# A written-out order of some 4,400 steps: the centroids' normalisation split into its single instructions, and the first 700 entries put in another order

## The chip, the cores and the metric

The kernel runs on one core of one Trainium2 chip, as one program and one launch. The metric is the time of one execution on the device, in microseconds (us), as the median of several runs.

The engines are called as in the profile: PE is TensorE, DVE is VectorE, ACT is ScalarE, POOL is GpSimd, and SP is SyncE, which here issues every transfer between memory and the chip.

## The reference

What is computed is an attention whose queries see only keys of the same cluster, and behind it a layer with a rational function between two matrix products. Cut to what matters:

```python
q_n, k_n, c_n = (each row divided by its norm + 1e-6)            # centroids: 8 heads x 16 clusters x 64
q_assign = argmax(q_n @ c_n.T);  k_assign = argmax(k_n @ c_n.T)  # per head
scores = q @ k.T / 8, -1e9 where q_assign != k_assign            # 4 batches, 8 heads, 768 x 768
x = softmax(scores) @ v                                          # heads side by side: 3072 x 512
h = x @ w_in                                                     # 512 -> 2048
g = (a0 + a1 h + a2 h^2 + a3 h^3) / (1 + |b0||h| + |b1|h^2 + 1e-6)
out = g @ w_out                                                  # 2048 -> 512
```

## The kernel before

Heads are worked in pairs: 4 batches of 4 pairs. For a pair, `prep` loads q and k, scales them by powers of two, splits them into a high and a low half of 16 bits (tiles `tk1`, `tq1`), turns them (`sk1`, `sq1`), multiplies them with the centroids (`ptl`), and finds each row's cluster as a one-hot row (`mx`, `df`, `mxi`, `oh`). The one-hot rows go into second tiles (`tk2`, `tq2`), which are turned too (`sk2`, `sq2`); a score is one product of the first tiles plus one of the second. For the pair 0 of batch 0 PE does the turning; for the others a transfer does.

Batch 0 works in `attend_keys`: a first pass of scores (`s`) gives each row's maximum (`top`, one DVE reduction over 768 values for each of 12 score tiles of a pair), a second pass (`z`) gives the scores with keys in rows, exponentials go to `at`, and `px` is the product with the values (tile `rv`). During batch 0 the two weight matrices are also loaded in 32 pieces (`rwi`, `rwo`), decoded on ACT (`mwi`, `gwi`, ...) and DVE (`wwi`, `wwo`), given their sign on POOL, scaled and split (`win`, `wout`). Behind that come the matrix products of the layer (`ph`, `po`) of one batch beside the attention of the next.

The centroids come once, ahead of all: one load (`craw`), squares and their sum (`csq`, `css`), a logarithm and an exponential on ACT, two steps of a root iteration and a division on DVE (`cn`, `cr`, `cnrm`), a turn on PE (`ctp`), and three instructions that write the parts of 16 bits (`cen`) that `ptl` reads.

Nothing is scheduled at run time. Each step calls `op(...)`, which only adds its function to a list; the table `ORDER` (line 63) names the places of that list, and `emit` calls them in that order. So each engine gets its instructions, and SP its transfers, in the order of the table. A step with several instructions, as the normalisation's, can't be parted by the table. The number that stands beside each engine's name in `op` is not used by it.

Each engine works off its own row and waits where a tile is not ready. Raw weights, and the values for their largest entry (`rvm`), share two buffers; `rk` and `rq` have one each, so that a pair's keys are loaded when the pair before has read its own.

"Warm" groups (`warm`, 16 of 8 products of 128x128 on a constant tile) have no result that is used; they are entries of the table like others.

Of the kernel before, what the change touches and what calls it, by code (L numbers as in the profile page):

```python
# [19 lines left out]
P = 128  # L20
# [42 lines left out]
72 73 4424 4421 4423 74 75 4435 4427 76 40 41 42 43 44 45 4429 4425 4422 371 370 373 4436 4428 375 376 4430  # L63
369 368 374 3 4 5 377 382 383 384 389 378 379 6 4434 380 381 385 386 387 388 390 397 12 13 392 393 400 77 34
35 36 38 37 39 7 8 9 4432 4426 399 398 394 396 402 391 395 10 11 28 29 30 31 401 403 404 32 33 519 518 521 523
524 405 46 50 47 48 525 530 406 531 407 532 408 516 517 522 526 527 528 4431 49 51 537 538 529 372 66 70 67
410 533 534 535 536 540 411 413 412 409 414 416 78 79 415 539 68 69 71 541 52 53 80 81 542 82 83 419 420 417
418 421 422 643 644 545 646 431 648 84 85 86 546 649 54 423 55 87 544 88 89 14 15 642 641 647 16 17 424 427
428 547 548 650 655 441 656 549 442 657 662 429 430 443 90 550 551 444 432 445 91 552 553 543 554 433 437 438
434 651 446 447 425 426 652 448 18 520 1 19 20 92 93 56 57 462 463 466 467 468 469 449 450 663 451 21 22 464  # L70
653 654 452 658 110 111 112 659 465 113 114 115 439 440 435 436 660 453 454 455 661 456 60 62 63 457 458 104
105 106 459 108 107 109 665 666 470 471 472 460 461 556 555 557 558 473 667 474 122 123 124 480 482 481 483
569 570 125 126 127 484 485 23 24 561 562 575 576 0 670 116 25 117 118 119 664 120 121 565 566 498 499 500 501
671 672 673 674 669 26 2342 2343 94 573 574 486 487 58 27 675 676 128 129 668 677 678 679 571 572 475 567 568
# [12 lines left out]
264 265 244 807 245 246 214 247 815 816 808 266 267 268 212 269 270 1358 1356 216 217 252 272 250 720 721 722
248 271 273 604 809 810 1357 734 735 723 724 829 830 1359 831 1360 274 275 276 832 770 833 1361 834 1362 835
175 277 1363 736 737 2 278 279 210 1366 1367 750 294 298 295 1364 296 297 299 725 748 749 751 726 727 738 739
740 741 1365 742 251 752 753 1368 754 755 280 281 836 843 743 306 310 1369 61 179 282 283 728 729 744 284 285  # L90
332 254 213 333 334 135 307 308 309 837 841 842 844 211 745 215 1497 335 336 337 338 339 340 341 342 312 313
314 315 316 290 317 756 757 758 855 856 838 1370 1371 1372 1373 1374 759 343 286 344 760 1375 345 1376 1377
839 840 857 858 859 761 762 763 1495 300 301 304 1496 1501 1498 1500 302 303 1296 1297 845 846 860 847 1379
1378 1382 1380 1502 861 862 346 1503 1505 347 1504 1506 1507 1508 1509 253 848 873 311 305 318 319 849 348 877
292 293 1513 1514 1510 287 1511 1512 320 321 874 288 289 875 876 322 323 1515 291 349 350 351 352 353 354 1516
355 356 324 1298 1299 863 864 878 325 357 358 850 851 852 359 360 361 879 880 1383 1381 1387 1388 1395 1396
865 866 328 1389 326 249 1390 327 1391 867 329 1397 1392 1393 764 765 1398 1399 881 882 883 884 885 868 869
870 1403 1404 362 363 364 853 854 1400 1401 1300 1301 1518 1517 1519 1520 365 366 367 1521 1522 1405 1302 1303
1304 886 887 1411 1412 1305 1306 1645 1644 1647 1649 1406 1407 888 1650 871 1523 1524 1413 1307 1308 1414 1415
255 1309 1310 1408 1409 1394 1351 1402 1416 1417 1410 1643 1418 1642 1384 891 892 893 894 330 1651 1653 1431  # L100
1432 1311 1433 897 898 899 1423 1424 895 896 1312 1313 1314 1434 900 901 902 1435 903 904 1315 1316 1526 1317
1385 1386 907 908 910 909 911 1654 912 1436 1437 331 1655 1425 923 924 925 746 1426 1427 926 927 928 929 913
914 1428 1429 940 941 943 942 1648 915 1430 1499 1447 1448 1449 905 933 747 872 930 1318 1525 944 945 1439
1440 916 946 947 1319 1652 917 1419 1420 1421 1422 1450 1451 1656 1657 1441 1442 1443 918 2346 1452 1527 2344
1453 1454 889 1444 973 974 976 956 948 1660 931 975 919 920 1445 1529 1459 1460 1461 1658 932 1661 977 978
1462 1463 957 959 1467 1468 960 1464 1465 921 906 979 980 934 935 936 1469 949 950 1470 1471 958 989 990 992
991 622 937 1472 962 963 961 995 996 1475 1476 1477 1659 1662 1473 1478 964 922 993 994 951 1479 1480 1005
1006 1007 1483 1484 1485 1663 1481 952 953 1008 1009 1486 1487 1010 1446 2345 1438 1455 1456 1457 1458 938 939
1488 1489 981 965 966 967 982 1011 1530 1466 1528 1534 1535 1536 954 1542 1543 1544 1664 968 969 970 890 983
1537 1538 2347 1665 1666 1667 1668 1669 1320 2348 1482 1545 1546 984 1539 1540 1547 1548 1026 1027 1028 1029  # L110
1030 1031 997 1032 1042 1043 1045 998 1044 1550 1551 1552 1558 1559 1560 1046 999 1000 1553 1554 1012 1670
1033 1531 985 986 1561 1532 1533 1555 1556 1059 1060 1062 1063 1562 1047 971 1048 1049 1490 955 972 1791 1789
1793 1549 1792 1794 1563 1013 1034 1061 1015 1065 1671 1673 1570 1571 1572 1035 1564 1064 1001 1573 1574 1474
1491 1492 1493 1586 1587 1014 1494 1036 1575 1576 1588 1108 1109 1796 1797 988 1111 1112 1050 1589 1590 1798
1800 1801 1790 1795 1037 1578 1579 1591 1592 1799 1113 1066 1067 1052 1541 1565 1672 1321 1322 1593 1676 1674
1677 1557 1577 1646 1580 1323 1581 1002 1124 1051 1125 1127 1582 1583 1802 1324 1016 1017 1018 1019 1110 1053
1606 1607 1608 1068 987 1003 1584 1128 1038 1039 1609 1610 1594 1595 1126 1803 1611 1612 1129 2349 1596 1075
1076 1078 1077 1069 1325 1070 1597 1598 1130 1131 1054 1055 1056 1599 1807 1614 1615 1616 1804 1081 1082 1617
1004 1091 1092 1094 1079 1805 1600 1080 1618 1619 1020 1022 1093 1326 1327 1114 1328 1329 1330 1808 1622 1623
1624 1097 1098 1115 1625 1566 1567 1620 1806 1809 1095 1096 1626 1627 1021 1675 1681 1682 1683 2350 1024 1684  # L120
1099 1601 1585 1628 1613 1629 1071 1072 1101 1685 1810 1141 1142 1630 1631 1041 1040 1686 1687 1083 1568 1569
1084 1085 1116 1143 1147 1689 1690 1331 1144 1145 1146 1086 1100 1102 2394 1812 1811 1691 1692 1693 1103 1632
# [1742 lines left out]
```

## Time and profile before

| | |
|---|---|
| median of 3 runs | 882.0 us (881.77 to 883.29) |
| the profiled execution | 883.15 us, of which 881.4 us are its span from the first to the last instruction |
| PE busy | 856.7 us (97% of the span) |
| DVE busy | 814.1 us (92%) |
| ACT busy | 783.9 us (89%) |
| POOL busy | 516.9 us (59%) |

The shares are averages over stages with different limits. The change lies in the first 131 us of the span, so what counts is which engine sets the pace there; a busy PE is not PE at its peak, since ends of matmuls are modelled.

### The profile page before, as it was taken

How to read it: one execution, taken by the hardware profiler on the slowest of the kernel's cores; microseconds unless marked ns; L12 is line 12 of the kernel's file. 1: busy time of each engine (PE TensorE's matmuls, PEld its weight loads, DVE VectorE, ACT ScalarE, POOL GpSimd, SP SyncE). 2: the span in 40 equal slices, each digit the busy share in tenths (PEclk: the TensorE clock that was granted, in tenths of full speed). 3: DMA queues.
4: the chain of work that ended last, by engine and by line, in shares of the span. 5: the costliest groups of instructions: out<-in, count | busy, mean ns of one | idle time of the engine just before them, and what ended most of it. 6: DMA issues, size and time to landing. Idle time of an engine off the chain costs nothing.

```text
span 881.4 us, 20941 instructions
## 1 busy us (share of the span) xinstructions
PE 856.7 (97%) x7893; PEld 595.3 (68%) x7893; DVE 814.1 (92%) x1627; ACT 783.9 (89%) x1482; POOL 516.9 (59%) x515
## 2 busy tenths in 40 slices
PE   7799999989999999999999999999999999999997
PEld 6577777757666676676766666676766666766654
DVE  6999998999999999999999999999999997879784
ACT  7698899999999999999999999999998988875752
POOL 3433445447687666667667566657674755345563
PEclk8899999999999999999999999999999999999999
DMA  7898757849989999889799999988987984330000
GB/s 230 238 244 196 188 178 198 177 94 204 174 155 180 197 164 186 172 141 228 162 182 202 172 179 183 157 177 155 167 152 142 146 154 78 76 59 1 25 25 25
DMA packets 353014, 135.77 MB, mean 154 GB/s; under 512 B 327824, under 2 KB 344208, under 8 KB 352912
## 3 DMA queue, kind: packets, MB, share of 16 engines
q1 hardware_dynamic: 352912, 134.42, 75.3%
q8 instruction: 62, 1.02, 0.5%
q14 instruction: 40, 0.33, 0.1%
HBM read 41.98 MB, written 6.29 MB: 55 GB/s over the span
## 4 chain that ended last, share of the span: by engine, by line
PE 52%; DVE 20%; ACT 17%; issue 6%; POOL 4%; DMA 0%; SPq 0%; ACTq 0%; DVEq 0%; POOLq 0%
PE po L1772 18%; PE ph L1623 18%; PE s L1254 6%; PE px L1334 5%; ACT s L420 4%; DVE s L1283 3%; DVE ah L1314 3%; ACT u L420 3%; ACT ah L420 3%; DVE top L1407 2%; ACT at L420 1%; DVE s L1742 1%; ACT t L420 1%; DVE t L1641 1%; PE ptl L1149 1%
## 5 line engine op out<-in xcount | busy, mean ns | idle before, releaser
L1623 PE MATMUL ph<-x,win 128*128 128x256 f16 x2304 | 267.5, 274 | 2.4 <-DVE t L1648 2.4
L1772 PE MATMUL po<-wout,g 128*128 128x512 f16 x1152 | 265.6, 379 | 0.0
L1623 PEld LDWEIGHTS <-win 128*128 128x128 f16 x2304 | 224.7, 98 | 43.2 <-DVE t L1648 4.2
L1772 PEld LDWEIGHTS <-g 128*128 128x128 f16 x1152 | 111.5, 98 | 120.8 <-issue 2.4
L1761 POOL TENSOR_TENSOR g<-t,u 128x512 f16<-128x512 f32 x84 | 113.1, 1348 | 82.8 <-DVE t L1754 52.0
L1314 DVE SCALAR_TENSOR_TENSOR ah<-s,su,ah 128x768 f16<-128x768 f32 x144 | 143.6, 1012 | 6.9 <-ACT ah L420 6.0
L1283 DVE TENSOR_SCALAR_CACHE_REDUCE s<-s,cc 128x768 f32<-128x768 f32 x144 | 144.5, 1018 | 5.0 <-PE s L1254 4.4
L420 ACT ACTIVATE ah<-s,su 128x768 f16<-128x768 f32 x144 | 126.4, 896 | 11.1 <-DVE su L1302 10.2
L420 ACT ACTIVATE s<-s,nm 128x768 f32<-128x768 f32 x144 | 125.9, 874 | 9.9 <-DVE s L1283 8.6
L1254 PE MATMUL s<-sk,sq 128*128 128x384 f16 x576 | 113.7, 326 | 2.3 <-DVE ah L1314 1.7
L1688 POOL TENSOR_TENSOR s<-s,u 128x512 f32<-128x512 f32 x69 | 91.6, 1332 | 31.9 <-ACT s L420 28.2
L1254 PEld LDWEIGHTS <-sq 128*128 128x128 f16 x576 | 53.0, 99 | 45.1 <-DVE ah L1314 12.8
L1334 PE MATMUL px<-at,vhi 128*64 128x256 f16 x864 | 73.7, 275 | 0.1
L1641 DVE SCALAR_TENSOR_TENSOR t<-ph,gk,t 128x512 f32<-128x512 f32 x84 | 62.3, 742 | 5.4 <-ACT t L420 5.2
L420 ACT ACTIVATE t<-ph,gk 128x512 f32<-128x512 f32 x84 | 65.1, 776 | 2.3 <-PE ph L1623 2.3
L1648 DVE SCALAR_TENSOR_TENSOR t<-t,gk,ph 128x512 f32<-128x512 f32 x84 | 62.2, 742 | 2.0 <-ACT u L420 0.8
L1742 DVE SCALAR_TENSOR_TENSOR s<-s,g 128x512 f32<-128x512 f32 x84 | 61.1, 727 | 1.1 <-POOL g L1717 0.5
L420 ACT ACTIVATE u<-ph,gk 128x512 f32<-128x512 f32 x84 | 57.5, 686 | 4.6 <-PE ph L1623 1.9
L420 ACT ACTIVATE u<-s,cq 128x512 f32<-128x512 f32 x84 | 60.1, 721 | 0.0
L1334 PE MATMUL px<-at,vlo 128*64 128x256 f16 x432 | 59.8, 273 | 0.0
L1748 POOL TENSOR_TENSOR t<-t,s 128x512 f32<-128x512 f32 x28 | 37.7, 1345 | 34.4 <-DVE s L1742 26.8
L1334 PEld LDWEIGHTS <-vhi 128*64 128x64 f16 x864 | 45.4, 110 | 12.3 <-issue 7.3
(237 smaller groups left out, 1572.8 us busy)
## 6 DMA issues: line engine op xcount, KB each, us to landing
rwo<-in_moe_w_out_dram SPq DMA_DIRECT2D x16, 512.0 KB, 4.0
rwi<-in_moe_w_in_dram SPq DMA_DIRECT2D x16, 512.0 KB, 4.1
rk<-in_k_dram SPq DMA_DIRECT2D x32, 192.0 KB, 3.8
rq<-in_q_dram SPq DMA_DIRECT2D x32, 192.0 KB, 3.8
rvm<-in_v_dram SPq DMA_DIRECT2D x16, 384.0 KB, 4.0
rv<-in_v_dram SPq DMA_DIRECT2D x16, 384.0 KB, 4.4
out_dram<-ob SPq DMA_DIRECT2D x24, 256.0 KB, 2.9
sq<-sq SPq DMA_DIRECT2D x12, 192.0 KB, 3.5
```

The lines of the kernel that those rows point to most:

```text
L420: lambda: nc.scalar.activation(out=out(), in_=in_(), func=func, **{a: (x() if callable(x) else x) for a, x in kw.items()}),
L1254: nc.tensor.matmul(sc.ap[:, i, :SH], lhsT=st["q" + x].ap[:, j, t, :], rhs=st["k" + x].ap[:, j, ks, :].rearrange("p t c -> p (t c)"), start ...
L1283: lambda nm=nm, view=view: ts(out=view(), in0=view(), scalar1=cc.ap[:, 0:1], scalar2=None, op0=ALU.mult, op1=ALU.min, accum_out=nm.ap),
L1314: lambda part=part, view=view, su=su: stt(out=part(1), in0=view(), scalar=su.ap, in1=part(0), op0=ALU.mult, op1=ALU.subtract),
L1334: nc.tensor.matmul(px.ap[j * D : (j + 1) * D, :], lhsT=vv.ap[:, j, kt, :], rhs=at[j].ap[:, p_, kt].rearrange("p t c -> p (t c)"), start=(i ...
L1623: nc.tensor.matmul(ph.ap[:, fi * TW : (fi + 1) * TW], lhsT=win[:, wpart, c, f * P : (f + 1) * P], rhs=xs[c].ap[:, xpart], start=(i == 0), ...
L1641: lambda t=t, h=h, ph=ph, col=col: stt(out=t[h].ap, in0=ph.ap, scalar=col("rho")(), in1=t[h].ap, op0=ALU.mult, op1=ALU.mult),
L1648: lambda t=t, h=h, ph=ph, col=col: stt(out=t[h].ap, in0=t[h].ap, scalar=col("a1")(), in1=ph.ap, op0=ALU.add, op1=ALU.mult),
L1688: lambda uv=uv, sv=sv: nc.gpsimd.tensor_tensor(out=sv(), in0=sv(), in1=uv(), op=ALU.mult),
L1742: lambda sv=sv, g16=g16: stt(out=sv(), in0=sv(), scalar=1.0 + 1e-6, in1=g16(0), op0=ALU.add, op1=ALU.mult),
L1761: lambda tv=tv, uv=uv, g16=g16, e=(nc.vector if kshare("gld", b, i_) else nc.gpsimd): e.tensor_tensor(out=g16(1), in0=tv(), in1=uv(), op=A ...
L1772: nc.tensor.matmul(po[ti].ap, lhsT=g16(gg)[:, c0 : c0 + P], rhs=wout[:, wpart, f, :], start=(i == 0 and f == 0), stop=(i == 2 and f == NF ...
```

## The change

There are two parts. The first takes the normalisation apart: what was one entry of 11 instructions becomes 11 entries, and the entry that writes `cen` becomes three. What is computed, and by which instructions, stays.

```diff
-    def centroid_norm():
-        ts(out=cn.ap, in0=cn.ap, scalar1=2.0 ** -15, scalar2=None, op0=ALU.mult)
-        for _ in range(2):
-            nc.vector.reciprocal(out=cr.ap, in_=cn.ap)
-            stt(out=cn.ap, in0=css.ap, scalar=cr.ap, in1=cn.ap, op0=ALU.mult, op1=ALU.add)
-            ts(out=cn.ap, in0=cn.ap, scalar1=0.5, scalar2=1e-30, op0=ALU.mult, op1=ALU.max)
...
-    dve(2230, centroid_norm, [cn, css, craw], [cn, cr, cnrm], V0)
+    def cdve(ns, fn, r, w):
+        dve(ns, fn, r, w, V0)
+
+    cdve(2231, lambda: ts(out=cn.ap, in0=cn.ap, scalar1=2.0 ** -15, scalar2=None, op0=ALU.mult), [], [cn])
+    for _ in range(2):
+        cdve(2232, lambda: nc.vector.reciprocal(out=cr.ap, in_=cn.ap), [cn], [cr])
...
-    dve(750, centroid_parts, [ctp], [cen], V0)
...
+    cdve(751, lambda: ts(out=cen.ap[:, 0], in0=csrc(), scalar1=C_SCALE, scalar2=None, op0=ALU.mult), [ctp], [cen])
+    for i in range(2):
+        cdve(
+            752,
...
-72 73 4424 4421 4423 74 75 4435 4427 76 40 41 42 43 44 45 4429 4425 4422 371 370 373 4436 4428 375 376 4430
+4440 4437 3 4 4436 5 6 7 8 9 10 11 12 13 4438 4435 4441 4443 4448 4433 4447 4442 4434 4439 84 85 86 87 88 52
```

The diff also adds other forms of the argmax and of the turning (`hsplit`, `half`, `evd`). They are chosen by entries of the table `K` that are not there, before and after, so that none of them is built.

The second part is the table. Each engine has the same instructions as before, and from some place on in the same order: DVE from row 277 of 1,475, ACT from row 172 of 1,289, POOL and SP from row 65, PE from a row past some 920 of its 7,000 pairs of weight load and product. On DVE and ACT these places lie at 127 to 128 us in the trace of before. What moves at the very start is shown engine by engine.

On SP, at the start of the program, the transfers stood so before (`rwo`, `rwi`: raw weights; `rk`, `rq`: keys and queries; `craw`: centroids; `rvm`, `rv`: values):

```order
L434 DMA rwo_1_120<-in_moe_w_out_dram 128x1024
L434 DMA rwi_2_174<-in_moe_w_in_dram 128x1024
L434 DMA rk_0_211<-in_k_dram 128x384 x2
L434 DMA rq_0_247<-in_q_dram 128x384 x2
L434 DMA craw<-in_centroids_dram 128x64
L434 DMA rvm_0_301<-in_v_dram 128x2x384
```

and stand so now:

```order
L434 DMA craw<-in_centroids_dram 128x64
L434 DMA rwo_1_250<-in_moe_w_out_dram 128x1024
L434 DMA rwi_2_259<-in_moe_w_in_dram 128x1024
L434 DMA rk_0_275<-in_k_dram 128x384 x2
L434 DMA rq_0_294<-in_q_dram 128x384 x2
L434 DMA rvm_0_327<-in_v_dram 128x2x384
```

The centroids' load went from the fifth place to the first; the two pieces of weights still stand ahead of the first keys. Further on, the load of the first pair's values (`rv` of pair 0) went from the 12th place to the 22nd, behind the last `rvm` of batch 0.

On DVE, behind the constants at the start, stood (`peaks<-kt`: the largest sum of squares of the keys; `ksc`: the keys' scale):

```order
L569 TENSOR_SCALAR wwo_1_151<-mwo_1_122 128x512
L576 SCALAR_TENSOR_TENSOR wwo_1_151<-rwo_1_120,wwo_1_151 128x512
L569 TENSOR_SCALAR wwi_2_178<-mwi_2_176 128x512
L576 SCALAR_TENSOR_TENSOR wwi_2_178<-rwi_2_174,wwi_2_178 128x512
L1026 TENSOR_REDUCE peaks<-kt_0_235 1x1
L455 TENSOR_TENSOR csq<-craw 128x64
L456 TENSOR_REDUCE css<-csq 128x1
L1038 TENSOR_SCALAR ksc_0_260<-kb_0_258 128x1
```

and now, from the same place on behind `csq`, `css`, three instructions on `cn` and a reciprocal:

```order
L473 SCALAR_TENSOR_TENSOR cn<-css,cr,cn 128x1
L478 TENSOR_SCALAR cn<-cn 128x1
L470 RECIPROCAL cr<-cn 128x1
L583 TENSOR_SCALAR wwo_1_254<-mwo_1_252 128x512
L590 SCALAR_TENSOR_TENSOR wwo_1_254<-rwo_1_250,wwo_1_254 128x512
L583 TENSOR_SCALAR wwi_2_263<-mwi_2_261 128x512
L473 SCALAR_TENSOR_TENSOR cn<-css,cr,cn 128x1
L590 SCALAR_TENSOR_TENSOR wwi_2_263<-rwi_2_259,wwi_2_263 128x512
L478 TENSOR_SCALAR cn<-cn 128x1
L480 TENSOR_SCALAR cn<-cn 128x1
L481 RECIPROCAL cr<-cn 128x1
L485 TENSOR_SCALAR cnrm<-craw,cr 128x64 x2
```

The whole normalisation went ahead of `peaks<-kt`; before, all but its first instructions stood 17 rows further on, behind a third weight piece. On ACT the two instructions on `cn` went from the 13th place to the first behind the table load. On PE 10 warm groups stood ahead of the first `kt` before, and 13 stand there now; of the others one stood at about 24.5 us before, and two stand behind the turning of `tq1` now.

On POOL, further on, stood (`tq<-oh`: the one-hot rows into `tq2`):

```order
L585 TENSOR_TENSOR wwi_0_383<-wwi_0_383,gwi_0_438 128x512
L585 TENSOR_TENSOR wwi_3_458<-wwi_3_458,gwi_3_454 128x512
L1192 TENSOR_SCALAR tq_0_366<-oh_0_469 128x12x48
L585 TENSOR_TENSOR wwo_0_551<-wwo_0_551,gwo_0_501 128x512
L585 TENSOR_TENSOR wwo_2_576<-wwo_2_576,gwo_2_581 128x512
```

and now:

```order
L599 TENSOR_TENSOR wwi_0_393<-wwi_0_393,gwi_0_449 128x512
L1299 TENSOR_SCALAR tq_0_348<-oh_0_487 128x12x48
L599 TENSOR_TENSOR wwi_3_468<-wwi_3_468,gwi_3_470 128x512
L1188 COPY tk_1_550<-mrow 128x12x16
L1191 MEMSET tq_1_577 128x12x16
```

The first pair's one-hot rows passed one product of weights and signs. In the same way PE now turns `tq2` of pair 0 ahead of `tk2`, and DVE writes the one-hot rows of `tk2` ahead of the low half of the second pair's keys.

## Rows read from the trace of the kernel before

**Rows 1.** Busy time of each engine in three stretches of the span.

```profile
core 0: us, PE busy (x) PEld busy (x) DVE busy (x) ACT busy (x) POOL busy (x), PEclk, DMA share, GB/s
...
5.30:32.28 26.98, 19.00 (x221) 15.85 (x219) 22.86 (x68) 21.96 (x39) 10.37 (x10) 0.75 0.75 229
32.28:131.00 98.72, 95.72 (x1160) 69.61 (x1159) 96.42 (x213) 85.57 (x159) 40.54 (x41) 1.00 0.81 208
...
180.00:881.40 701.40, 692.13 (x5831) 471.37 (x5829) 649.33 (x1221) 626.63 (x1188) 440.46 (x414) 1.00 0.75 141
```

**Rows 2.** The page's chain that ended last, shares of the span by engine.

```profile
PE 52%; DVE 20%; ACT 17%; issue 6%; POOL 4%; DMA 0%; SPq 0%; ACTq 0%; DVEq 0%; POOLq 0%
```

**Rows 3.** Timeline of the first 10 us: start, duration, engine, instruction, idle before.

```profile
3.56 0.45 SPq L434 DMA_DIRECT2D craw<-in_centroids_dram  x1
4.66 0.67 ACT L420 ACTIVATE mwo<-rwo 128x512 f32<-128x512 f32 x1 [2.65 <-DMA rwo<-in_moe_w_out_dram]
...
8.18 0.27 PE L1024 MATMUL kt<-ident,sumk 128*1 128x128 f32 x1
...
8.48 0.28 DVE L1026 TENSOR_REDUCE peaks<-kt 1x1 f32<-1x128 f32 x1 [0.62 <-PE kt L1024]
...
8.82 0.38 PE L1028 MATMUL kb<-peaks,ones 128*128 128x1 f32 x2
...
9.54 0.15 DVE L1038 TENSOR_SCALAR ksc<-kb 128x1 int32<-128x1 int32 x1
```

**Rows 4.** The chain in order of time: warm groups ahead of `kt`.

```profile
5.03 0.84 PE warm-39.94_163 L797 x8
...
7.65 0.45 PE warm-39.93_226 L797 x8
```

**Rows 5.** Timeline from 13 to 33 us, the first pair's way to its scores.

```profile
13.78 0.43 ACT L420 ACTIVATE cn<-cn 128x1 f32<-128x1 f32 x2
14.11 1.49 ACT L1009 ACTIVATE sk<-tk 128x768 f16<-128x768 f16 x2
14.18 0.69 DVE L576 SCALAR_TENSOR_TENSOR wwi<-rwi,wwi 128x512 int32<-128x512 int32 x1
...
16.18 0.67 ACT L420 ACTIVATE mwi<-rwi 128x512 f32<-128x512 f32 x1
...
16.74 0.82 ACT L1009 ACTIVATE sq<-tq 128x768 f16<-128x768 f16 x1
...
18.86 1.06 PE L1149 MATMUL ptl<-cen,sq 128*128 128x16 f16 x24 [0.45 <-DVE cen L488]
...
20.67 0.56 DVE L1163 TENSOR_REDUCE mx<-ptl 128x24 f32<-128x384 f32 x1
...
23.29 0.56 DVE L1173 TENSOR_TENSOR oh<-df,mxi 128x384 f16<-128x384 bf16 x1
...
24.78 2.21 POOL L585 TENSOR_TENSOR wwi<-wwi,gwi 128x512 f32<-128x512 f32 x1 [2.73 <-DVE wwi L576]
...
27.08 0.67 POOL L1192 TENSOR_SCALAR tq<-oh 128x576 f16<-128x576 f16 x1
...
31.43 1.46 PE L1397 MATMUL s<-sk,sq 128*128 128x384 f16 x8 [0.38 <-ACT sq L1009]
...
32.28 2.68 DVE L1407 TENSOR_REDUCE top<-s 128x1 f32<-128x768 f32 x3
```

**Rows 6.** Instructions on the tile `cn`: duration min/median/max in ns, first and last start.

```profile
L469 DVE SCALAR_TENSOR_TENSOR cn<-css,cr,cn x2: 220/676/1131, 15.2 to 16.7; 128x1 f32<-128x1 f32 x2
```

**Rows 7.** Waits of DVE between 0 and 33 us: total, times, longest.

```profile
DVE tk L1107 <- PE tk L991: 1.1, 1, 1.1
```

**Rows 8.** The tile `rv`, 0 to 60 us: its loads, its reader, time to landing.

```profile
L1512 PE MATMUL px<-at,rv x24: 379/379/430, 48.2 to 50.6; 128*64 128x256 f32 x24
L434 SPq DMA_DIRECT2D rv<-in_v_dram x2: 432/450/467, 16.3 to 37.5; - x2
...
DMA to landing us min/median/max: 5.0/5.6/6.2
```

More of the change, by code (lines that the diff above doesn't have):

```diff
@@ L973, in prep @@
         pet = keymajor and hp in kn("pet", ())
+        hsplit = kn("hsplit") and quick and pet
+        parts = (
+            {x: [Buf(lambda h=h, t=tm[x]: t.ap[:, h], None, 0, False) for h in range(2)] for x in ("k1", "q1")}
+            if hsplit
+            else {x: [tm[x]] for x in ("k1", "q1")}
+        )
         q2 = []
@@ L985, in turn_pe, with blocks @@
             src = tm[x]
-            sc = bank([P, 2, 1024], F16, "s", f"t{x}_{n}", 2)
-            def blocks():
-                for h in range(2):
+            one_bank = not (hsplit and x in ("k1", "q1"))
+            if one_bank:
+                sc = bank([P, 2, 1024], F16, "s", f"t{x}_{n}", 2)
+            def blocks(sc, hs):
+                for h in hs:
                     for t in range(NT):
@@ L993, in blocks @@
                         )
-            op("PE", 771, blocks, [src], [sc], u, chain=x)
+            if one_bank:
+                op("PE", 771, lambda sc=sc: blocks(sc, range(2)), [src], [sc], u, chain=x)
             for h in range(2):
+                if not one_bank:
+                    o = x == "q1" and not h
+                    sc = bank([P, 2, 1024], F16, "o" if o else "s", f"t{x}_{n}_{h}", 1 if o else 2)
+                    op("PE", 772, lambda sc=sc, h=h: blocks(sc, (h,)), [parts[x][h]], [sc], u, chain=x)
                 if x == "q2":
@@ L1004, in turn_pe @@
                     out = lambda h=h: st[x].ap[:, h].rearrange("p t c -> p (t c)")
-                    src_ = lambda h=h: sc.ap[:, h, : NT * P]
+                    src_ = lambda h=h, sc=sc: sc.ap[:, h, : NT * P]
                     w, co = [st[x]], [st[x]]
+                if h and x in kn("evd", ()):
+                    op(
+                        "DVE", 894, lambda out=out, src_=src_: nc.vector.tensor_copy(out=out(), in_=src_()),
+                        [sc], w, u, co=co,
+                    )
+                    continue
                 op(
@@ L1083, in prep @@
             one = tm[nm + "1"]
+            for h in range(2) if hsplit else ():
+                act(
+                    931, lambda nm=nm, hi=hi, h=h: tm[nm + "1"].ap[:, h, :, hi * D : (hi + 1) * D],
+                    lambda nm=nm, h=h: raw[nm].ap[:, h], AF.Identity,
+                    [raw[nm], sc], [parts[nm + "1"][h]], u, scale=lambda sc=sc: sc.ap[:, 1:2],
+                )
+                dve(
+                    1472,
+                    lambda nm=nm, sc=sc, hi=hi, lo=lo, h=h: stt(
+                        out=tm[nm + "1"].ap[:, h, :, lo * D : (lo + 1) * D], in0=raw[nm].ap[:, h], scalar=sc.ap[:, 1:2],
+                        in1=tm[nm + "1"].ap[:, h, :, hi * D : (hi + 1) * D], op0=ALU.mult, op1=ALU.subtract,
+                    ),
+                    [raw[nm], sc], [parts[nm + "1"][h]], u, n=1,
+                )
+            if hsplit:
+                dve(
+                    730, lambda nm=nm, hi=hi: nc.vector.tensor_copy(out=cols(nm + "2", 0), in_=cols(nm + "1", hi)),
+                    parts[nm + "1"], [tm[nm + "2"]], u,
+                )
+                continue
             act(
@@ L1140, in prep @@
             (turn_pe if pet else turn)(x, vt + kb("p2", b, 2))
-        G = 4 * NT
-        ptl = misc([P, G, NCL], F32, f"ptl{n}")
-        def logits():
-            for g, (x, part) in enumerate((("q1", 1), ("q1", 1), ("k1", 2), ("k1", 2))):
-                for t in range(NT):
-                    for i in (0, part):
-                        nc.tensor.matmul(
-                            ptl.ap[:, g * NT + t, :], lhsT=st[x].ap[:, g % 2, t, :], rhs=cen.ap[:, i, h0 + g % 2, :],
-                            start=(i == 0), stop=(i != 0),
-                        )
@@ L1199, in prep @@
+        (halves if kn("half") and quick and keymajor else whole_argmax)()
         for x in ("k2", "q2"):
```

173 lines of the change are left out of this document (123 added, 50 removed), and 384 rows, old and new, of the table ORDER.

## The prediction, made before the changed kernel ran

> **What bounds the kernel now.** I read the busy time by stretch first. From 180 us on PE is busy for 692.1 of 701.4 us: the long second part is PE's. Between 32.28 us, where the first row maximum (`top`) is taken, and 131 us it is DVE that is full, 96.42 of 98.72 us, with ACT at 85.57 [rows 1]. Between 5.3 and 32.28 us no engine is full: DVE idles 4.12 of 26.98 us, ACT 5.02, and the granted clock of TensorE is 0.75 of the upper level on average against 1.00 afterwards [rows 1]. That is a chain of single steps from the first loads to the first scores, and nearly all that the table moves at the front lies in it. The page's chain that ended last gives transfers and their queue 0% of the span [rows 2]: work is handed from engine to engine, so a start that comes earlier by some time, with the same order behind it, should hand that time on to the end.
>
> In the timeline the reader is to follow one pair's way. ACT's first work waits for a weight piece until 4.66 us, the keys' sum is turned on PE at 8.18, their scale `ksc` starts at 9.54 [rows 3]. The centroids' division runs on DVE behind ACT's logarithms, from 15.2 us [rows 6], and PE waits 0.45 us for `cen` before the products `ptl` at 18.86 [rows 5]. Then `mx` at 20.67, the one-hot rows `oh` done at 23.85, their copy into `tq2` only at 27.08 because POOL first does a sign product of 2.21 us, the products that wait for ACT's turned `sq2` at 31.43, and `top` at 32.28 [rows 5].
>
> **The change, step by step.** *The centroids' load in front.* Its issue takes 0.45 us [rows 3], so every load behind it starts that much later and ACT's first work moves from 4.66 to about 5.1. When the centroids land alone is shown nowhere: not before their issue ends, some 1.2 us, and hardly later than the 4.66 at which a weight piece of 16 times their size was there. Either way the first DVE instructions fit ahead of the first weight piece's decoding or delay it by half a microsecond, and neither sets what follows, because of the next step. I put it at nothing; its cover is PE's warm groups.
>
> *Thirteen warm groups ahead of `kt`.* The tenth ends at 7.65 + 0.45 = 8.10 [rows 4]. Three more at 0.45 end at 9.45; `kt` starts there and not at 8.18: +1.27 us. The keys' sums, there by 8.18 before, would be ready by 8.18 + 0.45 = 8.63 at the latest, so this wait is new. DVE gets to `peaks` about then too: two weight pieces and the rest of the normalisation stand ahead of it. Part comes back: before, `peaks` at 8.48 and `ksc` at 9.54 are 1.06 apart, though `kb` was done at 9.20 [rows 3], since the squares of the centroids stood between. Now `ksc` starts at 9.45 + 0.30 to `peaks`, + 0.34 to `kb`, + 0.40 = 10.49. **First term: +0.95 us** on the keys' scale and all that hangs on it: the scaled keys on ACT, their low half on DVE, the turning on PE.
>
> *The normalisation off the path.* From there to the turned queries ACT works without a gap, so it is late by 0.95, but its two instructions on `cn` (start to next start 0.33) have gone to the front, and the decoding of a weight piece that stood between the halves of `sq` (start to next start 0.56) now stands behind them [rows 5]. The second half of `sq` ended at 17.56; it now ends at 17.56 + 0.95 - 0.33 - 0.56 = 17.6, say 17.7 since the halves also wait for PE. `cen` is then long there. Before, from the start of `ptl` to `mx` 1.81 us went by [rows 5]; so `mx` starts at about 19.6 to 19.7 against 20.67. DVE must by then have decoded the weight piece that ACT gives it at 17.7 + 0.67 = 18.4; the longer of its two instructions takes 0.69 [rows 5], I count 1.2 for both, which ends at 19.6 too. **Second term, with the first in it: `mx` 1.0 us earlier.**
>
> *One-hot rows of the queries past a sign product.* `oh` ends 3.18 us behind `mx` with the same instructions between, so at about 22.8. POOL copies at once, 4 us sooner than at 27.08, and PE turns `tq2` ahead of `tk2`. But DVE has the same instructions between `mx` and the first `top` as before, 11.61 us from start to start. What can shrink there is a wait: 1.06 us until `tk2` was turned [rows 7]. It goes, but PE now comes to `qb` of the second pair only behind the turning of `tq2`, and DVE waits for that instead, 0.6 us by the place in the rows, and ACT has the second pair's queries between the evacuations. Bounds: all of 1.06 gained, or nothing. I take 0.2, nearer to nothing, since a new wait of the same kind stands in its place. **Third term: -0.2.**
>
> *The stretch from 32.28 to 131 us.* The instructions are the same, in another order, and DVE is the bound. It idles 2.30 us in all [rows 1], so no order gains more than that, unless fewer DVE instructions collide with POOL's; on the other side I let the idle time double, +2.3. I take 0: DVE's row is about as tight as it can be, and nothing in the rows tells which order is better.
>
> *The first pair's values ten places later.* Their load was issued at 16.3; now it stands just ahead of the second pair's, which went out at 37.5, and lands 5.0 to 6.2 us later, at 43.7 at the latest. `px` reads it at 48.2 [rows 8], or 47 if all is a microsecond earlier. Three microseconds cover it; beyond them each one would go straight to `px`. It costs nothing.
>
> *From 131 us on* the order is the same and the shift is handed on whole.
>
> **Sum:** -1.0 - 0.2 + 0 = -1.2 us. On the profiled execution's own time, 883.15 us (span 881.4), that is 882.0; that execution lies 1.15 above the median of the three runs, 882.0, so I forecast the median at 880.8 us.
>
> *A rule weighed against the rows.* The root step on `cn` took 1131 ns once and 220 ns the other time [rows 6], on 128 single values. The slow one lay beside a sign product on POOL. The Trainium skill (SBUF — State Buffer, Who interferes with whom) says that a DVE instruction with two inputs in SBUF and a POOL instruction that reads SBUF exclude each other for a whole instruction. The trace agrees for this pair. By that rule the second root step and the two of `cnrm`, which now run near 7.6 to 9.4 us beside the first sign product, could be held up by as much as 0.9 us more, and the sum would be -0.3 instead of -1.2. I keep -1.2, because the root step comes ahead of the product's start and `cnrm` has one tensor input.
>
> **The rivals.** *More than that is gained* (the stretch of DVE gets tighter too). For it: 2.30 us idle between 32.28 and 131 us, and one-hot rows of the queries ready 4 us sooner. Against it: 97.7% is hard to better. With half to all of the 2.3 and of the 1.06 gained, 878.6 to 880.2; middle 879.4.
>
> *The gain is lost in DVE's stretch.* For it: DVE waits there now for ACT and POOL in 2.3 us, and an order that was arranged around other times may wait for 1.2 more. Then 882.0 (881.6 to 882.6).
>
> *The keys' scale sets the start.* If ACT's saving of 0.33 and 0.56 is eaten by waits for PE's turning, the +0.95 of the first term stays, plus up to 0.3 for the queries behind it: 883.0 to 883.3, slower than before. It decides if `mx` starts after 21.0 us. Against it: the 0.89 are ACT's own instructions and ACT had no gap there.
>
> *TensorE's clock stays low into the first scores* (slower). The warm groups have moved to the front, so PE has longer holes between 15 and 28 us. Warm groups took 0.84 us in one part and 0.45 in the other [rows 4], a ratio of 1.9 between the two levels of 1.2 and 2.4 GHz. A score tile of four products, half of the 1.46 us of eight or 0.73 [rows 5], would take 1.4, against 0.9 (2.68 for three) for the maximum on DVE: PE would set the pace, 0.5 us a tile. From six tiles on that outweighs the gain by more than 0.2%; twelve give +4.8 us: 884 to 886. The Trainium skill (TensorE: Matmul & The Clock Gate, Part 1) says that the clock is gated by how busy TensorE has been; this trace agrees, 0.75 on average in the broken stretch and 1.00 in the full one. Against it: PE turns and sums weights densely just ahead of the scores, as before.
>
> *The change doesn't do what it says* is only true in that the keys and queries aren't loaded right behind the centroids: two weight pieces still stand ahead of them, which is in the sum.
>
> **How the numbers follow.** A measurement of this kernel tells 0.2%, 1.76 us, from no change; the edges are 880.24 and 883.76. Forecast (880.2 to 881.6) 0.36; more gained 0.35; lost in the stretch 0.10; keys' scale 0.08; clock, or another collision of that size, 0.11. So faster 0.35, same 0.36 + 0.10 + 0.08 = 0.54, slower 0.11. The likeliest single case is the forecast, 880.8 with its own range of 880.2 to 881.6. The range that leaves out 0.1 at each end goes from 878.8, in the better rival, to 883.7, at the edge of the clock's case.
>
> **What would show it.** `kt` at about 9.4, `ksc` at 10.5; `mx` near 19.7 and `top` near 31.1; no wait of PE for `cen`; `tq2` turned before 25 us; DVE's idle time between the first `top` and 131 us still about 2.3 us; the same shift of about 1.2 us at 180 us and at the end. The prediction is wrong if DVE's idle time in its stretch moves by more than a microsecond, if the keys' scale isn't late, or if the granted clock behind 30 us isn't 1.00.

## The result, and the profile after

The changed kernel takes 887.0 us (median of 4, 885.33 to 887.41) against 882.0 beside it: 1.0051 times as long, 95% interval 1.0036 to 1.0065. Measured a second time, beside three of the experiments, it was 886.6 against 883.2, 1.0038 (1.0024 to 1.0052). It is slower by 3.4 to 5 us, outside the range that was given and on the other side of the forecast.

The first two stretches of [rows 1], after the change:

```profile
core 0: us, PE busy (x) PEld busy (x) DVE busy (x) ACT busy (x) POOL busy (x), PEclk, DMA share, GB/s
5.30:32.28 26.98, 17.11 (x205) 14.65 (x202) 22.83 (x55) 20.96 (x35) 9.96 (x11) 0.68 0.62 194
32.28:131.00 98.72, 94.71 (x1095) 67.69 (x1096) 95.29 (x210) 82.66 (x153) 38.15 (x37) 0.98 0.81 210
```

In the first stretch DVE is as busy as before, 22.83 against 22.86 us, with 55 instructions in place of 68. Eight of the thirteen that are missing have only moved ahead of 5.3 us, with the normalisation, so the count alone proves little. From `mx` to the first `top`, however, DVE has the same 28 instructions in both kernels; that stretch before, then after (the 29th instruction of the first row is the end of an earlier one):

```profile
20.67:32.28 11.61, 8.04 (x64) 6.32 (x64) 9.91 (x29) 8.31 (x13) 6.11 (x5) 0.61 0.72 199
21.44:34.62 13.18, 7.27 (x51) 5.65 (x52) 12.22 (x28) 9.34 (x16) 6.77 (x7) 0.61 0.64 167
```

DVE is busy for 12.22 us there against 9.91, at the same granted clock of TensorE, 0.61: its instructions have become longer, it does not wait more. That is the sight from which the rest follows. The timeline after the change, DVE's long rows with POOL's beside them (start, duration):

```profile
8.38 1.26 POOL L599 TENSOR_TENSOR wwi<-wwi,gwi 128x512 f32<-128x512 f32 x1 [5.11 <-DVE cn L478]
8.60 0.27 PE L1057 MATMUL kt<-ident,sumk 128*1 128x128 f32 x1
8.71 2.40 DVE L485 TENSOR_SCALAR cnrm<-craw,cr 128x64 f32<-128x64 f32 x2
9.61 1.26 POOL L599 TENSOR_TENSOR wwo<-wwo,gwo 128x512 f32<-128x512 f32 x1
10.84 0.28 DVE L1059 TENSOR_REDUCE peaks<-kt 1x1 f32<-1x128 f32 x1
11.82 0.16 DVE L1071 TENSOR_SCALAR ksc<-kb 128x1 int32<-128x1 int32 x1 [0.70 <-PE kb L1061]
...
17.51 1.27 POOL L599 TENSOR_TENSOR wwi<-wwi,gwi 128x512 f32<-128x512 f32 x1 [6.44 <-DVE wwi L590]
17.55 1.45 DVE L1160 COPY tq<-tq 128x768 f16<-128x768 f16 x1
...
21.44 0.56 DVE L1270 TENSOR_REDUCE mx<-ptl 128x24 f32<-128x384 f32 x1
...
25.89 1.32 POOL L599 TENSOR_TENSOR wwi<-wwi,gwi 128x512 f32<-128x512 f32 x1
...
26.00 2.02 DVE L1153 SCALAR_TENSOR_TENSOR tk<-rk,ksc,tk 128x768 f16<-128x768 f32 x1
...
31.31 1.90 POOL L599 TENSOR_TENSOR wwo<-wwo,gwo 128x512 f32<-128x512 f32 x1
32.00 1.49 DVE L583 TENSOR_SCALAR wwo<-mwo 128x512 int32<-128x512 int32 x1
...
34.62 0.95 DVE L1516 TENSOR_REDUCE top<-s 128x1 f32<-128x768 f32 x1
```

Each of the long DVE rows begins while a sign product of POOL runs and ends behind it: `cnrm` behind two of them (10.87), the copy of `tq`, the scaling of `tk`, the decoding of `wwo`. In the kernel before the first three had nothing of POOL ahead of them:

```profile
17.55 0.42 DVE L474 TENSOR_SCALAR cnrm<-craw,cr 128x64 f32<-128x64 f32 x2
17.88 0.35 DVE L1107 COPY tq<-tq 128x768 f16<-128x768 f16 x1
...
24.57 1.00 DVE L1100 SCALAR_TENSOR_TENSOR tk<-rk,ksc,tk 128x768 f16<-128x768 f32 x1
```

The decoding took 0.65 there. After the change `kt` was turned at 8.87, but `peaks`, next in DVE's row, had to wait for `cnrm`, and with it the keys' scale.

I added up what each DVE instruction takes beyond the shortest durations of the same instruction in all the traces of this study, where that is over 0.25 us. Up to 36 us it is 1.4 us (2 instructions) before and 5.7 us (6) after: two `cnrm`, the copy, the scaling and the decoding above, and one step of `tk` beside POOL's one-hot copy (0.49). `top` comes at 34.62 against 32.28 [rows 5], 2.34 us later.

Behind it the shift grows to 4.2 us at the last `top` of batch 0 (136.35 against 132.11). From the first `top` to the last DVE is busy for 98.3 us against 97.5 and idle for 3.4 against 2.3. It waited 0.2 us for score tiles there before, and now:

```profile
DVE top L1516 <- PE s L1506: 2.0, 3, 1.3
```

At 180 us the profiled execution gets 1.5 us back: in the execution of before the granted clock was 0.50 from 179.8 to 183.2 us, in this one it did not fall there. Nine of the sixteen traces of this study have such a fall between 179 and 188 us; seven, the two of the changed kernel among them, have none. Whether the change has a part in that was not tested. This execution is the fastest of the four, so its span understates the loss.

A second trace of the changed kernel (after_again) divides the loss otherwise: its first `top` comes at 33.89, 1.61 us late, and its last at 137.18, 5.07 late, with 3.0 us of waits for score tiles and a granted clock of 0.50 from 23.0 to 40.0 us.

### The profile page after: what moved, and what is told of

Read it like the earlier page. It is cut to its first block, busy times and chain, and to the rows that moved or that the text cites. A ratio compares the mean times of both kernels' runs of the same rounds, so it can differ in the third digit from the quotient of the medians.

```text
span 883.5 us, 20940 instructions
## 1 busy us (share of the span) xinstructions
PE 856.6 (97%) x7893; PEld 594.6 (67%) x7893; DVE 818.4 (93%) x1627; ACT 783.3 (89%) x1482; POOL 515.5 (58%) x515
## 3 DMA queue, kind: packets, MB, share of 16 engines
q8 instruction: 62, 1.02, 0.4%
## 4 chain that ended last, share of the span: by engine, by line
PE 65%; DVE 15%; ACT 10%; issue 5%; POOL 3%; DMA 1%; SPq 0%; ACTq 0%; DVEq 0%; POOLq 0%
PE po L1881 20%; PE ph L1732 19%; PE s L1363 7%; PE px L1443 6%; PE s L1506 3%; DVE ah L1423 3%; ACT s L420 3%; PE px L1621 2%; DVE s L1392 2%; PE z L1600 2%; ACT u L420 2%; ACT ah L420 2%; PE ptl L1256 1%; PE px L1627 1%; DVE s L1851 1%
```

## The experiments

Three theories stood against each other. A: the loss is made in the front, by DVE instructions that stand still beside POOL's sign products, and by the warm groups ahead of `kt`. B: the changed order behind the first scores makes it. C: TensorE's clock, lower in the front and low again among the first scores, makes it. (The expectation of front_new still counts the front's clock to A.)

Times are medians, beside the kernel before on the same chip; "ratio" is with its 95% interval.

| | time, us | before | ratio |
|---|---|---|---|
| front_new | 885.7 | 882.7 | 1.0032 (1.0020 to 1.0045) |
| front_old | 883.4 | 882.7 | 1.0011 (1.0000 to 1.0022) |
| nosign_new | 882.2 | 882.7 | 0.9993 (0.9984 to 1.0001) |
| nosign_old | 880.7 | 882.7 | 0.9974 (0.9963 to 0.9985) |
| cnrm_late | 885.0 | 882.9 | 1.0025 (1.0015 to 1.0035) |
| two_back | 883.9 | 882.9 | 1.0015 (1.0006 to 1.0023) |
| warm_more | 887.0 | 882.9 | 1.0042 (1.0029 to 1.0056) |
| old_early | 884.1 | 882.9 | 1.0015 (1.0004 to 1.0026) |
| apart | 883.2 | 883.2 | 1.0000 (0.9990 to 1.0011) |
| apart_old | 883.3 | 883.2 | 1.0001 (0.9989 to 1.0012) |
| warm_back | 887.6 | 883.2 | 1.0050 (1.0036 to 1.0064) |
| after_again | 886.6 | 883.2 | 1.0038 (1.0024 to 1.0052) |
| apart_load | 884.6 | 883.0 | 1.0020 (1.0005 to 1.0035) |
| old_load | 883.8 | 883.0 | 1.0010 (0.9994 to 1.0025) |

The diffs of orders are given in the names of the steps, not as numbers of the table.

**Front or stretch.**

```diff
front_new: -ORDER = changed table
           +ORDER = changed table up to the first score product, then the old table's rest
front_old: -ORDER = changed table
           +ORDER = old table up to the third row maximum, then the changed table's rest
```

> The changed order up to the first score product, the old order behind it. Theory A (the loss is made in the front, by DVE instructions that stand still beside POOL's sign products and by the TensorE clock that is low because of the holes in front): 885 to 887.5 us, DVE's first row maximum near 34.6 us. Theory B (the new order from the first score to 131 us makes the loss): 881.5 to 883.5 us.

> The old order up to the third score tile, the changed order behind it. Theory A: 881 to 883 us, as before. Theory B: 884.5 to 887.5 us, with DVE idle 2 us or more between the first row maximum and 131 us.

The changed front alone costs 3.0 us, the changed rest alone 0.7 (interval 0 to 1.9). In the stretch from 32.28 to 131 us DVE's wait for score tiles goes with the new rest, not with the front; first front_new, then front_old:

```profile
DVE top L1516 <- PE s L1506: 0.2, 1, 0.2
```

```profile
DVE top L1516 <- PE s L1506: 1.3, 1, 1.3
```

front_new lies in the range of theory A; front_old, 883.4, lies above A's range and below B's. By these times theory A holds for most of the loss, theory B for a part that is barely measurable. How the loss is divided differs between executions: in the trace of after_again 3.5 of the 5.1 us arise behind the first `top`.

**The sign products left out.**

```diff
         for i in ORDER:
-            self.ops[i]()
+            if i not in (45, 51, 57, 63, 83, 89, 95):
+                self.ops[i]()
```

> The changed kernel without the first seven sign products on POOL (four pieces of the first weight matrix, three of the second keep the sign they have, so the layer's values are other ones; all else is the same). If DVE loses its time beside these products, cnrm takes 0.42 instead of 2.40 us, the copy of tq 0.35 instead of 1.45, the scaling of tk 1.00 instead of 2.02, and the time falls by 3.5 to 5.5 us, to 881.5 to 883.5. If the low TensorE clock is what costs, at most 1.5 us less: 885.5 or more.

> The kernel before without the same seven sign products. In its trace one DVE instruction of the front stood beside such a product (a root step, 1.13 instead of 0.22 us). Collisions as the cause: 880.5 to 882 us, and the changed kernel without them within 1 us of this one. Clock or order as the cause: 880.5 to 882 us too, but the changed one stays 3 us or more above it.

The timeline of nosign_new has the short durations back:

```profile
8.60 0.42 DVE L486 TENSOR_SCALAR cnrm<-craw,cr 128x64 f32<-128x64 f32 x2
10.41 0.28 DVE L1060 TENSOR_REDUCE peaks<-kt 1x1 f32<-1x128 f32 x1 [1.39 <-PE kt L1058]
...
16.69 0.35 DVE L1161 COPY tq<-tq 128x768 f16<-128x768 f16 x1
...
25.09 1.00 DVE L1154 SCALAR_TENSOR_TENSOR tk<-rk,ksc,tk 128x768 f16<-128x768 f32 x1
...
30.18 0.43 DVE L584 TENSOR_SCALAR wwo<-mwo 128x512 int32<-128x512 int32 x1
...
31.79 2.73 DVE L1517 TENSOR_REDUCE top<-s 128x1 f32<-128x768 f32 x3
```

Without the products the two orders differ by 1.4 us (882.15 and 880.72), with them by 3.4 to 5. The products are thus behind more than half of the loss, but not all: the expectation of within 1 us was missed, though not by much, for the intervals of the two ratios just touch. These runs also take the products' own time off POOL, so by themselves they can't tell the standstills from that; cnrm_late and apart below keep every product. What is left shows in the second row: with `cnrm` out of the way `peaks` waits 1.39 us for `kt`, which stands behind thirteen warm groups. The clock has a part in it: it rose at 7.5 us in this execution, at 4.8 in that of nosign_old. The old order, too, gains 2 us without the products; its slow root step takes 0.22.

**`cnrm` moved, then the warm groups too.**

```diff
cnrm_late, DVE:
 cr<-cn
-cnrm<-craw,cr x2
 peaks<-kt ... ksc ... peaks<-qt ... qsc ... cc, qsc
+cnrm<-craw,cr x2
 tk<-rk,ksc,tk
 (PE: ctp behind qb; DVE: the first cen behind the copies of tk and tq)
two_back, PE, on top of it:
-13 warm groups, kt, kb, qt, qb
+10 warm groups, kt, 1 warm group, kb, qt, 1 warm group, qb, 1 warm group
```

> The changed order with the two divisions cnrm, the turn ctp and the first cen moved behind the queries' scale on DVE, so that the keys' maximum no longer stands behind cnrm. Theory A (cnrm, held 2.40 us beside POOL, is what makes the keys' scale late): peaks follows kt at once, ksc starts at 10.0 to 10.5 instead of 11.82, the time falls by 1.3 to 2 us, to about 885. Rival (the thirteen warm groups hold kt back anyway, the lower clock included): ksc at 11 or later, 886 to 887.

> As cnrm_late, and three of the thirteen warm groups moved back behind kt, qt and qb. If the warm groups ahead of kt cost time of their own, 0.5 to 1.5 us less than cnrm_late, with kt at 8.2 to 8.6. If they don't, within 0.4 us of cnrm_late.

cnrm_late's timeline:

```profile
9.32 0.27 PE L1057 MATMUL kt<-ident,sumk 128*1 128x128 f32 x1
9.63 0.28 DVE L1059 TENSOR_REDUCE peaks<-kt 1x1 f32<-1x128 f32 x1 [0.89 <-PE kt L1057]
10.38 0.16 DVE L1071 TENSOR_SCALAR ksc<-kb 128x1 int32<-128x1 int32 x1 [0.47 <-PE kb L1061]
12.28 0.40 DVE L485 TENSOR_SCALAR cnrm<-craw,cr 128x64 f32<-128x64 f32 x2
...
15.90 1.45 DVE L1160 COPY tq<-tq 128x768 f16<-128x768 f16 x1
```

and two_back's:

```profile
9.05 0.28 DVE L1059 TENSOR_REDUCE peaks<-kt 1x1 f32<-1x128 f32 x1 [0.15 <-PE kt L1057]
9.80 0.16 DVE L1071 TENSOR_SCALAR ksc<-kb 128x1 int32<-128x1 int32 x1 [0.47 <-PE kb L1061]
...
18.83 0.56 DVE L1270 TENSOR_REDUCE mx<-ptl 128x24 f32<-128x384 f32 x1
...
32.01 0.95 DVE L1516 TENSOR_REDUCE top<-s 128x1 f32<-128x768 f32 x1
```

Both steps came as theory A has them: 1.1 to 2.3 us for `cnrm` (ratio from 1.0038 or 1.0051 to 1.0025), another 0.9 for the warm groups (to 1.0015). The intervals of one step and the next overlap; that of both together lies clear of the changed kernel's. The second pays only once the first is done, as the next run shows.

**The warm groups alone.** As two_back, with `cnrm` left where the change put it.

> The changed order with only the three warm groups moved back behind kt, qt and qb. Theory A (cnrm covers the warm groups' cost: peaks can't start before cnrm ends): within 0.5 us of the changed kernel, 886.3 to 887.3. If the warm groups cost by themselves: 885.8 or less.

No gain: 887.6 us, 1.1 above the changed kernel beside it (886.6) and a little above the expected 886.3 to 887.3. The row of `cnrm` says why nothing is won; `kt` is turned at 9.20, and `peaks` waits for DVE itself:

```profile
8.93 0.27 PE L1057 MATMUL kt<-ident,sumk 128*1 128x128 f32 x1 [0.79 <-issue]
9.10 2.41 DVE L485 TENSOR_SCALAR cnrm<-craw,cr 128x64 f32<-128x64 f32 x2
11.24 0.28 DVE L1059 TENSOR_REDUCE peaks<-kt 1x1 f32<-1x128 f32 x1
```

**The clock among the first scores.**

```diff
-'warm': 16
+'warm': 20
 PE: wig<-wwi
+2 warm groups
 s (first score tile)
+2 warm groups
 win<-wia
```

> The changed order with four more warm groups, two ahead of the first score tile and two behind it, where PE waited 0.71 and 1.16 us. Theory C (the clock that falls again among the first scores costs time): granted clock 1.00 from the first score on, DVE's 2.0 us of waits for score tiles gone, 885 to 885.7 us. Rival (those waits are made by what stood still before): 886.3 to 887.3.

No gain: 887.0. In the profiled execution the granted clock is 1.00 from 34.2 us on, where the changed kernel's was 0.50 from 35.0 to 38.4, and still DVE waits for score tiles:

```profile
DVE top L1516 <- PE s L1506: 1.6, 3, 0.8
```

So the low clock among the first scores is not what costs the time here. Of the 2.0 us, the 1.3 of front_old at the full clock belongs to the new order. For the clock ahead of the scores two traces speak: from `mx` to the first `top` nosign_new takes 11.26 us at a granted clock of 0.55, where the changed kernel takes 13.18 at 0.61, and cnrm_late has its first `top` 1.5 us earlier (33.10) although its clock from 5.3 to 32.28 us is lower, 0.64 against 0.68. What the clock costs in after_again, where it was 0.50 until 40.0 us, is not shown.

**Only the centroids early, in the old order.**

```diff
SP:  +craw first                     (was behind rq)
DVE: +csq, css, cn ... cnrm x2, then wwo<-mwo     (was behind the scales)
PE:   kt, +ctp, warm group, kb
DVE:  cc, qsc, +cen x3, tk<-rk,ksc,tk
```

> The old order with the one thing moved that the split allows: the centroids' load first, their whole normalisation ahead of the first weight piece, the turn behind kt, cen behind the queries' scale. If taking 3.2 us of DVE and two ACT instructions out of the way to the first scores is a gain by itself: 880.5 to 881.7 us. Rival (the instructions that move up behind POOL's sign product at 15.0 to 16.3 us, the copies of tq and tk, stand still there instead): 882 to 883 us, as before.

Slower than before by 1.3 us (0.4 to 2.3), which neither side had. Its timeline shows the rival's standstill, and a wait that I had made myself by putting the turn ahead of `kb`:

```profile
10.24 0.16 DVE L1071 TENSOR_SCALAR ksc<-kb 128x1 int32<-128x1 int32 x1 [1.14 <-PE kb L1061]
...
17.35 1.27 POOL L599 TENSOR_TENSOR wwi<-wwi,gwi 128x512 f32<-128x512 f32 x1 [6.50 <-DVE wwi L590]
17.39 1.64 DVE L1160 COPY tk<-tk 128x768 f16<-128x768 f16 x1
...
21.68 0.56 DVE L1270 TENSOR_REDUCE mx<-ptl 128x24 f32<-128x384 f32 x1 [0.97 <-PE ptl L1256]
```

Before, the division stood between that sign product and the copies, and only its one root step of two inputs was caught. With the division gone the copies move up beside the product.

**The other standstills taken away by order.**

```diff
apart, on top of two_back:
DVE: tk, tq (scaled)  +copy tk, copy tq   wwi<-mwi, wwi<-rwi,wwi  -copy tk, copy tq   cen
DVE: oh  -wwi<-rwi,wwi   tk<-oh, tk<-rk,ksc,tk  +wwi<-rwi,wwi   peaks<-qt
DVE: wwo<-mwo  +copy tq   wwo<-rwo,wwo, wij  -copy tq   top
POOL: memset tq  -sign of wwo piece 0   sign of wwo piece 2  +sign of wwo piece 0
apart_old: apart up to the first score product, then the old table's rest
```

> As two_back, and the three DVE instructions that still stood still beside POOL's sign products are parted from them by order alone: the copies of tk and tq go ahead of a piece's decoding, the scaling of tk of the second pair ahead of the last step of another piece, one sign product behind the next one. Theory A: the copy of tq takes 0.35 instead of 1.45 us, tk 1.00 instead of 2.02, the decoding 0.43 instead of 1.49, and the time falls by 2 to 3 us against two_back, to 881 to 882. Rival (what is gained there is waited for elsewhere, on ACT or PE): 883.3 or more.

> As apart up to the first score product, the old order behind it. If the new order behind the first scores costs its 0.7 us (front_old): 0.5 to 1 us less than apart, 880 to 881.5. If not: as apart.

All standstills up to 36 us are gone (0.0 us by the sum above), and the time is that of the kernel before: 1.3 us better than two_back by the ratios, whose intervals just overlap, not 2 to 3. In apart's own trace the first `top` is 0.9 us ahead of the old kernel's (31.36), and DVE then waits for score tiles, while the granted clock is 0.50 until 36.5 us:

```profile
DVE top L1516 <- PE s L1506: 3.0, 5, 1.2
```

apart_old came out as apart, not the 0.5 to 1 us below it, so the 0.7 of front_old is not found again here. Where the rest went in the old order is seen in its trace, whose first row maximum comes 2.0 us ahead of the old kernel's:

```profile
30.28 2.68 DVE L1516 TENSOR_REDUCE top<-s 128x1 f32<-128x768 f32 x3
...
31.90 0.84 ACT L420 ACTIVATE tk<-rk 128x768 bf16<-128x768 f32 x1 [1.80 <-DMA sk<-tk]
...
34.41 0.66 ACT L420 ACTIVATE mwo<-rwo 128x512 f32<-128x512 f32 x1 [1.58 <-DMA rwo<-in_moe_w_out_dram]
...
35.11 0.43 DVE L583 TENSOR_SCALAR wwo<-mwo 128x512 int32<-128x512 int32 x1 [2.15 <-ACT mwo L420]
```

ACT waits for two transfers and DVE for ACT; at 35 us the lead is used up. Farther on chance takes another microsecond: a decoding that ran free in the old kernel falls beside a sign product.

```profile
68.93 1.28 POOL L599 TENSOR_TENSOR wwo<-wwo,gwo 128x512 f32<-128x512 f32 x1 [2.68 <-DVE wwo L590]
69.12 1.37 DVE L583 TENSOR_SCALAR wwo<-mwo 128x512 int32<-128x512 int32 x1 [0.34 <-ACT mwo L420]
```

**The late weight piece.**

```diff
SP: rk x2
+   rwo (fourth piece)
    turning transfer sk<-tk
    rv
-   rwo (fourth piece)
```

> As apart_old, with the load of one weight piece, the fourth of the second matrix, moved two transfers forward on SP, ahead of the turning transfer of the second pair's keys. In apart_old DVE reached its first row maximum at 30.28, 2.0 us before the old kernel, and then stood 2.15 us for this piece. If SP's row is what holds the piece back: that wait falls under 0.5 us and the time is 881 to 881.8, 1.5 to 2 below apart_old. If the piece's buffer or something behind it holds it: within 0.5 us of apart_old.

> The old order with the same load moved forward and nothing else: the old kernel does not wait for this piece, so 882.3 to 883.3, as before, in either theory.

The load is issued at 27.92 in place of 29.61, and nothing is won; at 884.6 us it is rather above apart_old:

```profile
27.92 0.33 SPq L434 DMA_DIRECT2D rwo<-in_moe_w_out_dram  x1
...
34.52 0.84 ACT L420 ACTIVATE tk<-rk 128x768 bf16<-128x768 f32 x1 [3.56 <-DMA sk<-tk]
...
36.05 0.43 DVE L583 TENSOR_SCALAR wwo<-mwo 128x512 int32<-128x512 int32 x1 [2.21 <-ACT mwo L420]
```

What came forward is paid by the turning transfer that now stands behind it: ACT waits 3.56 us for that and hands DVE the piece as late. The 16 DMA engines are full there, by the stretch of apart_old:

```profile
26.00:36.00 10.00, 7.68 (x57) 4.93 (x55) 7.52 (x17) 6.04 (x11) 3.53 (x4) 0.84 1.06 286
```

A share of 1.06 and 286 GB/s: it is not SP's order that holds the piece, at least not alone. That the transfers' sum is the limit is what the share suggests; no run took transfers away, so it stays open. old_load lies 0.9 us above the kernel before and above the 882.3 to 883.3 that was expected, with an interval that includes no change.

## Why the prediction was wrong

**The step that failed** is the one that put the centroids' instructions at nothing, and with it the place where a rule was weighed and set aside; the third term failed in the same way, by giving DVE's instructions between `mx` and `top` their old durations. "I keep -1.2, because the root step comes ahead of the product's start and `cnrm` has one tensor input": the root step did come ahead (7.41), but `cnrm`, the very instruction that was excused, stood still for 2 us. I had the price of the pair (0.9 us at most) from a single row [rows 6] and took only the half of the rule that fitted that row. The Trainium skill (SBUF — State Buffer, Who interferes with whom) says more than I weighed: copies and `tensor_scalar` in a two-port fast mode take the shared ports too, and whoever comes second waits for the whole instruction. This trace agrees: 1.45 against 0.35 us for a copy, 1.49 against 0.43 for a `tensor_scalar`; in which mode they ran it does not show. The scaling of `tk` reads two tensors from SBUF and so falls under the half that was weighed, but I looked for it at `cn` alone.

**The keys' scale, first term, +0.95.** It was 11.82 in place of 10.49. `kt` came at 8.60 in this execution and at 9.37 in the second one of the same kernel (forecast 9.45): the warm groups take 0.85 us each until the clock rises, and it rose at 4.3 and at 5.9 us. The mechanism was right and, with `cnrm` gone, its price too: cnrm_late has `ksc` at 10.38 against the forecast 10.49, and moving three groups back is worth 0.9 us. In the changed kernel `cnrm` covers it (warm_back): that `kt` came 0.85 us ahead of the forecast in the profiled execution was the clock's luck, and gained nothing.

**ACT's gain, second term, `mx` at 19.7.** It came at 21.44; with `cnrm` moved at 19.84, with the warm groups back at 18.83. PE does not wait for `cen` any more but for `sq`, as forecast. From `ksc` to `mx` the forecast has 9.2 us; it took 11.13 before, 9.62 in the changed kernel and 9.36 in nosign_new. So ACT's gain was right to 0.4 us, and `mx` is late because `ksc` is.

**Third term, -0.2, and the 0 of the stretch.** Behind `mx` the prediction had 11.4 us to the first `top`; it took 13.18. The wait of 1.06 us for `tk2` went and one of 0.68 for `qb` came in its place, as forecast. What failed is the busy time, with the scaling of `tk` (+1.02), the decoding (+1.09) and the step of `tk` (+0.49) held up, and a part of that covered. nosign_new needs 11.26. None of these three was seen: I read the order of each engine by itself and never laid POOL's row beside DVE's for the new times. By front_old the new rest costs 0.7 us (0 to 1.9), inside the +2.3 that I allowed; in the two traces of the changed kernel the time from the first `top` to the last is 1.9 and 3.5 us longer than before.

**The sum.** The forecast of -1.2 for `top` and 5.7 - 1.4 = 4.3 us of added standstills make +3.1; +2.34 was measured, the rest was covered by other waits. Taken step by step, the first `top` was forecast at 31.08 and came 3.54 us later: 1.33 of that up to `ksc`, 0.44 from there to `mx`, 1.77 from `mx` to `top`. Half of it thus lies in the third term, not at `cnrm`.

**"The shift is handed on whole"** failed as well, on the side of a gain: front_new's shift of 3.1 us at the last `top` is still 2.6 at the end, but apart_old's lead of 2.0 is lost within 5 us: the transfers that ACT waits for were issued no earlier than before (the turning of `tk` at 26.43 against 26.45, the weight piece at 29.61 against 29.09). In these runs a delay at the front went through to the end, and a lead did not. Without the standstills the forecast of the front would have been about right and would hardly have gained anything: nosign_new has its first `top` at 31.79, where 31.08 was forecast, and a time of 882.2 against 882.7, with an interval that includes no change.

**The rivals.** "The keys' scale sets the start" had the place and the outcome (slower, `mx` after 21.0, as its condition said) at 883.0 to 883.3, but named waits for PE's turning as the cause; the standstills were "another collision of that size" in the clock's case, 884 to 886, where 0.11 of the chance lay, and the 887.0 of the first measurement is above that too. The clock itself was lower than before, 0.68 against 0.75 in the front; raising it among the first scores gave nothing, and between 11 and 31 us it wasn't tried by itself. Two of the signs that the prediction named did show: DVE idles 3.43 us between 32.28 and 131 us in place of 2.30, and the granted clock behind 30 us was 0.50 for a while, from 35.0 to 38.4.

## What to carry to other kernels

Where DVE and POOL share a stretch, a new order must be read with both rows side by side: for each POOL product with operands in SBUF, ask which DVE instruction will start beside it, and add up to the product's remaining time if it is a copy, a `tensor_scalar` over more than single values, or takes two tensors from SBUF. An engine that is busy for longer with the same instructions is the sign of it. And before a lead is handed on to the end, look what the next stage waits for that the change does not bring forward.

## What the runs showed of the hardware

The standstills did not depend on size alone. A root step of 128 single values with two tensor inputs was held (1131 against 220 ns, [rows 6]), while the steps of `ksc`, single values with one tensor input, took 0.15 to 0.16 us beside a sign product in the kernel before (9.54 to 10.07, the product from 9.25 to 10.52), and row maxima that read scores from PSUM kept their 0.95 us. The sixteen traces together bear this out. Of the DVE instructions up to 131 us that began inside a sign product with at least 0.25 us of it to run, all 15 copies of `tk` and `tq` took over 0.15 us longer than their shortest durations, and so did 10 of 11 decodings, all 7 scalings of `tk`, all 3 root steps on `cn`, and all 7 of a `tensor_scalar` of 12 values a row (`tq<-rest`, 0.36 to 0.72 against 0.19). None of the 255 row maxima did, and none of the single-value instructions with one tensor input. The one wide `tensor_scalar` that was not held is `tk<-oh`, 4 of 4, each beside a product that had itself been held.

POOL pays as well: a sign product of 1.27 us took 1.90 to 2.21 beside such DVE work. The order of the two starts tells who pays: before, the scaling of `tk` began 0.21 us ahead of the product and kept its 1.00 us while the product took 2.21 [rows 5]; after, the product began 0.11 us ahead and took 1.32 while the scaling took 2.02.

Which of two instructions meets which is a matter of tenths of a microsecond: in apart_old and nosign_old the same decoding at 69 us stood still that ran free in the kernel before, in the same order. The kernel before itself was measured between 880.9 and 887.4 us in the course of the study, more than the differences of most runs; so each ratio rests on runs side by side.
